# The third block's softmax transposes on VectorE instead of TensorE, and its value products two steps later

## The chip, the core and the metric

The kernel runs on one core of one Trainium2 chip. The metric is the device time of one execution in microseconds (us); the kernel before is given by the median of three runs.

## The reference

Chunked attention over chunks of 64 tokens (8 batches, 8 heads, 576 tokens of 64 values each), followed by a gated feed-forward layer over all 4608 tokens. All is float32.

```python
# q, k, v: (8, 8, 576, 64), cut into 9 chunks of 64 tokens
scores = (q_c @ k_c.transpose) / sqrt(64)
scores = scores - max(scores, axis=-1)
attn = exp(scores)
attn = attn / (sum(attn, axis=-1) + 1e-9)
x = (attn @ v_c)                      # -> (4608, 512)
g = x @ w_gate                        # (512, 1536)
val = x @ w_val                       # (512, 1536)
out = (silu(g) * val) @ w_out         # (1536, 512)
```

## The kernel before

The 4608 tokens are worked on in nine blocks of 512 (`N`), one for each chunk position over all batches. For a block, the attention gives x, held transposed as [feature, token] and split into a high part and a low part (`xh`, `xl`), so that a product is made of three reduced-precision matmuls instead of one in full float32. The feed-forward layer runs in twelve steps over slices of 128 hidden features (`NF` = 12): a gate product and a value product, silu and multiplication to h, a split of h into `hh` and `hl` (`parts`: ScalarE casts in line 62, VectorE subtracts in line 63), and the projection (`project`, lines 544 to 546), twelve matmuls of 128x512 that add into four accumulators `ps_o`.

The orders of TensorE, ScalarE and VectorE are those in which the program is written; SP's queue, which starts the loads, is ordered by a planner with its own estimates of cost, once the opening stages are past.

Blocks 0 and 1 (`a0`, `a1`) go first. While the feed-forward steps of both are computed, the h of `a1` is written to memory and its projection is left for later. The change lies in the loop that does this projection. Its steps are counted by f from 0 to 11:

```python
    for f in range(NF):
        lag(*put.pop(0))
        fetch_o(f + 3)
        extra.get(f, lambda: None)()
        if f + 2 < NF:
            put.append((prepare(f), ready_o[f]))
```

- `lag` projects the item handed over one step earlier (step 0 projects nothing, so steps 1 to 11 are twelve matmuls each).
- `fetch_o` asks for the output weights of later steps (loads of `both`).
- `prepare(f)` splits a loaded h (`h_in`) into hh and hl, each of which has two buffers, so that the split at step f waits for the buffers of the item that is projected at step f + 1; it is itself projected at step f + 3. After each odd f it asks for the next `h_in` (line 966), whose two buffers come free with the splits.
- `extra[f]` holds the work for the third block, `nxt`, whose attention is done beside this projection. Before: exponents (steps 0, 1), sums and normalizing of the pairs 0 and 1 (steps 1, 2) and 2 and 3 (steps 3, 4), the loads of the values (5), the transposes of the probabilities (6, copies of pairs 2 and 3 in step 7), the value products `columns` (8), and the split of the result into `xh` and `xl` (`first`, line 622 on ScalarE, and `rest`, line 626 on VectorE; steps 8 to 10). Step 11 computes the scores of the fourth block into the PSUM banks (`ps_gv`, `ps_a`) that the columns used. Step 6 also asks for the queries and keys of that block, behind the last load of `h_in`.

Pairs are pairs of heads; a block has four. The transpose turns probabilities [query, key] into [key, query], which the value product needs. TensorE does it by sixteen matmuls of 128x128 with an identity (`turn_to`, line 454) into PSUM, and ScalarE copies the four results to SBUF (line 1023). Later blocks of this kernel turn theirs on VectorE already (class `Attn`, `turn`, line 355), by instructions that turn eight squares of 32x32 each. `columns` (line 468) takes the pairs 0 and 1 first, then 2 and 3: 64 matmuls of 64x64 each.

After this loop, the feed-forward steps of `nxt` begin.

Of the kernel before, what the change touches and what calls it, by code (L numbers as in the profile page):

```python
# [8 lines left out]
F32 = mybir.dt.float32  # L9
# [8 lines left out]
P = 128  # L18
C = 64
# [6 lines left out]
NP = H // 2  # L26
T = 4
N = T * P
# [5 lines left out]
def attn_then_gated_ffn(ctx: ExitStack, tc: tile.TileContext, qk, v, wgv, wo, out):  # L34
    nc = tc.nc
    const = ctx.enter_context(tc.tile_pool(name="const", bufs=1))
# [7 lines left out]
    ps_gv = ctx.enter_context(tc.tile_pool(name="ps_gv", bufs=2, space=bass.MemoryType.PSUM))  # L44
    ps_o = ctx.enter_context(tc.tile_pool(name="ps_o", bufs=T, space=bass.MemoryType.PSUM))
    ps_a = ctx.enter_context(tc.tile_pool(name="ps_a", bufs=2, space=bass.MemoryType.PSUM))
# [46 lines left out]
    class Up(Narrow):  # L93
# [27 lines left out]
        def upper(self):  # L121
            f = self.f
            self.w = const.tile([P, 2, 2 * NK * P], F32R, name="w", tag=f"w{f}")
            nc.scalar.copy(out=self.w[:, 0], in_=self.t)
            w_both.append(self.w)
            w_hi.append(self.w[:, 0].rearrange("p (g k m) -> p g k m", g=2, m=P))
            w_lo.append(self.w[:, 1].rearrange("p (g k m) -> p g k m", g=2, m=P))

        def lower(self):
            nc.vector.tensor_tensor(out=self.w[:, 1], in0=self.t, in1=self.w[:, 0].bitcast(F32), op=ALU.subtract)  # L130
# [6 lines left out]
    class Quarters:  # L137
# [5 lines left out]
        def sums(self, t, s=None, engine=nc.vector):  # L143
            if s is None:
                s = const.tile([P, 4, Q], F32, name="ts", tag="ts")
            self.s = s.rearrange("p i q -> p (i q)")
            t = t.rearrange("p (i q) -> p i q", q=Q)
            engine.tensor_tensor(out=s[:, 0:2], in0=t[:, 2:4], in1=t[:, 0:3:2], op=ALU.subtract)
            engine.tensor_tensor(out=s[:, 2], in0=t[:, 3], in1=s[:, 0], op=ALU.subtract)
            engine.tensor_tensor(out=s[:, 3], in0=t[:, 1], in1=s[:, 2], op=ALU.subtract)  # L150
# [24 lines left out]
    def moved(i):  # L175
        return f"w{(i + EARLY) % NF}"
# [74 lines left out]
    class Attn:  # L251
# [83 lines left out]
        def columns(self, v_t, pT, pool=ps_a, tag="ps_a", more=False):  # L335

            pT = pT.rearrange("p (u k) -> p u k", k=C)
            px = pool.tile([P, 2 * T, C], F32, name="px", tag=tag)
            for u in range(2 * T):
                for h in range(2):  # L340
                    r = slice(h * C, (h + 1) * C)
                    nc.tensor.matmul(px[r, u, :], v_t[r, u, :], pT[r, u, :], start=not more or u == 0, stop=True,
                                     skip_group_check=more)
            return px.rearrange("p u k -> p (u k)")

        def turn(self, p, j, parts=(0, 1)):


            if not hasattr(self, "turned"):
                self.turned = const.tile([P, NP, 2, T, C], F32, name="turned", tag=self.at)  # L350
            src = self.s[:, p:p + 2].rearrange("p a c h k -> p (a c) h k")
            for i in (2 * j + i for i in parts):
                for o in range(4):
                    to = 32 * (o ^ 2 * j)
                    nc.vector.transpose(  # L355
                        out=self.turned[to:to + 32, p:p + 2, j, :, 32 * (i % 2):32 * (i % 2) + 32],
                        in_=src[32 * i:32 * i + 32, :, o // 2, 32 * (o % 2):32 * (o % 2) + 32])
# [29 lines left out]
    class First(Attn):  # L387
# [18 lines left out]
        def load_v(self, p, t):  # L406
            nc.sync.dma_start(out=t, in_=v[:, p:p + t.shape[1], self.b])

        def exchange(self, t, to, copy=nc.gpsimd.tensor_copy):
            for h in range(2):  # L410
                copy(out=to[h * C:(h + 1) * C], in_=t[(1 - h) * C:(2 - h) * C])  # L411
# [79 lines left out]
    def save_o(f):  # L491
        nc.sync.dma_start(out=kept_o[f], in_=out_now[f].bitcast(F32))
# [31 lines left out]
    def gated(a, f):  # L524
        h = gate(a, f)
        times(h, value(a, f))
        return h
# [65 lines left out]
    w, o = up[0], down[0]  # L593
# [16 lines left out]
    for a, vs in ((a0, v0), (a1, v1)):  # L610
        for c in range(2):
            pool, tag = (ld, "v_t") if a is a0 else (wp, "wo")
# [114 lines left out]
    for do in opening.split():  # L727
# [14 lines left out]
        else:  # L742
            b, i = int(do[1]), int(do[2])
# [69 lines left out]
    for f in range(1, SEVEN):  # L813
        w, o = up[f + 1], down[f]
# [168 lines left out]
    nxt = First(2)  # L983
# [15 lines left out]
    z, two, px = {}, {}, {}  # L999
# [11 lines left out]
                    r, to = slice(h * C, (h + 1) * C), slice((1 - h) * C, (2 - h) * C)  # L1011
                    nc.sync.dma_start(out=two[p][to], in_=v[r, p, nxt.b])

    def turn():
        nxt.turned = const.tile([P, NP, N], F32, name="pT", tag="turned")
        for p in range(NP):
            pt[p] = (ps_a if p < 2 else ps_gv).tile([P, T, P], F32, name="pt", tag="ps_a" if p < 2 else "ps_gv")
            nxt.turn_to(p, pt[p])
        copy(0)

    def copy(p):
        for i in (p, p + 1):
            nc.scalar.copy(out=nxt.turned[:, i], in_=pt[i].rearrange("p m k -> p (m k)"))

    def columns():
        for p in (0, 2):
# [4 lines left out]
    def first(p):  # L1031
        for i in (p, p + 1):
            upper(nxt, px[p], i)

    def rest(p):
        for i in (p, p + 1):
            lower(nxt, px[p], i)

    pt = {}
    nxt.places()  # L1040

    extra = {0: lambda: nxt.exponents(0), 1: lambda: (nxt.exponents(2), sums(0)), 2: lambda: nxt.normalize(0, z[0]),
             3: lambda: sums(2), 4: lambda: nxt.normalize(2, z[2]), 5: load_v, 6: turn, 7: lambda: copy(2), 9: lambda: (first(2), rest(0)), 10: lambda: rest(2)}

    def scores(a, beside_pair=True, at=None, tiles=None):

# [175 lines left out]
    a, pair = nxt, []  # L1222
    queries = []

    def load_queries():
        with tc.issue_after(last_fetch[0]):
            queries.extend(pair[0].a[0].load_qk(p, 1, xs, tag) for p, tag in enumerate(("xh0", "xl0", "xh1", "xl1")))
# [1 line left out]
    extra[NF - 1] = lambda: scores(pair[0].a[0], False, tiles=(queries[:2], queries[2:]))  # L1229
    ask = extra[6]  # L1230
    extra[6] = lambda: (ask(), pair.append(Pair(3, moved(2))), load_queries())
    extra[8] = columns
    save_o(NF - 1)
    for f in range(NF):
        lag(*put.pop(0))
# [6 lines left out]
    c = pair.a[0]  # L1242
# [25 lines left out]
    for i in range(NF):  # L1268
        f = (i + EARLY) % NF
        h = gated(a, f)  # L1270
# [17 lines left out]
    for b in range(3, NB, 2):  # L1288
        pair.last = b + 2 == NB
        middle, behind, bursts, later = {}, {}, {}, {}  # L1290
        if not pair.last:
            n = Pair(b + 2, moved(11))
            c = n.a[0]
# [45 lines left out]
```

## Time and profile before

| | |
|---|---|
| median of three runs | 893.55 us (893.28 to 893.56) |
| the profiled execution | 893.09 us |
| its span, from the first to the last instruction | 890.9 us |
| TensorE busy | 880.8 us (99%) |
| VectorE busy | 547.6 us (61%) |
| ScalarE busy | 388.1 us (44%) |
| granted TensorE clock, mean | 0.999 |
| the loop of the change, from its first projection to the fourth block's scores | 186.1 to 222.2 us |

The rows below name an instruction by its start in us from the start of the span, its length, its engine (PE is TensorE, PEld its weight loads, DVE is VectorE, ACT is ScalarE, SPq the loads started by SP), its line in the kernel and its tiles, `out<-in`. In brackets stands the time in which the engine stood idle before it, and what ended that. Rows for a whole line give the durations as min/median/max in ns.

### The profile page before, as it was taken

What the parts mean: (1) busy time and instruction counts of PE and PEld (TensorE: products, weight loads), DVE (VectorE), ACT (ScalarE), POOL (GpSimd) and SP (SyncE); (2) the same over time, 40 slices, a digit from 0 to 9 for tenths busy, and PEclk for the clock granted to TensorE, in tenths of its full rate; (3) what the DMA queues carried; (4) which work ended last, traced back from release to release, by engine and by line L of the source; (5) the groups of instructions that cost most, each with busy time, mean ns of one, the idle gap of its engine ahead of it and who ended that gap; (6) DMA issues with size and microseconds to landing.
All of it is one profiled execution on the core that took longest, in us unless ns stands there. A gap on an engine that the chain in (4) does not pass through costs nothing.

```text
span 890.9 us, 14750 instructions
## 1 busy us (share of the span) xinstructions
PE 880.8 (99%) x6038; PEld 729.8 (82%) x6038; DVE 547.6 (61%) x830; ACT 388.1 (44%) x592; POOL 41.6 (5%) x33
## 2 busy tenths in 40 slices
PE   7999999999999999999999999999999999999998
PEld 6788888888888888888888888888888888888886
DVE  6888999673888656776753656767655533333332
ACT  5757777544433345225325444244325432223232
POOL 1200000000145110000000000000000000000000
PEclk9999999999999999999999999999999999999999
DMA  9667778889798877657577857575658575556651
GB/s 357 265 254 287 270 282 320 336 293 341 249 365 278 275 259 234 250 215 256 207 250 284 305 199 276 196 248 219 211 213 281 177 271 201 200 196 231 237 189 47
DMA packets 73314, 223.25 MB, mean 251 GB/s; under 512 B 30752, under 2 KB 31264, under 8 KB 59040
## 3 DMA queue, kind: packets, MB, share of 16 engines
q1 hardware_dynamic: 71664, 219.57, 67.8%
q10 hardware_dynamic: 1584, 2.75, 0.9%
q8 instruction: 47, 0.77, 0.3%
q14 instruction: 19, 0.16, 0.0%
HBM read 178.78 MB, written 43.52 MB: 250 GB/s over the span
## 4 chain that ended last, share of the span: by engine, by line
PE 94%; DMA 2%; DVE 2%; ACT 1%; POOL 1%; issue 0%; SPq 0%; ACTq 0%; DVEq 0%; POOLq 0%
PE ps_a L865 26%; PE ps_gv L865 20%; PE ps_gv L478 12%; PE ps_o L544 11%; PE ps_o L546 11%; PE ps_o L545 11%; DMA v_t<-in_v 2%; PE ps_a L290 2%; PE ps_a L368 1%; DMA qk_t<-in_qk 1%; PE ps_a L468 0%; POOL v_t L411 0%; DVE h L522 0%; PE ps_a L454 0%; POOL s_sb L449 0%
## 5 line engine op out<-in xcount | busy, mean ns | idle before, releaser
L865 PE MATMUL ps_a<-x,factors 128*128 128x512 f32 x864 | 219.2, 389 | 0.0
L865 PEld LDWEIGHTS ps_a<-x,factors 128*128 128x128 f32 x864 | 162.2, 188 | 33.7
L865 PE MATMUL ps_gv<-x,factors 128*128 128x512 f32 x648 | 164.4, 389 | 0.0
L865 PEld LDWEIGHTS ps_gv<-x,factors 128*128 128x128 f32 x648 | 121.6, 188 | 25.3
L544 PE MATMUL ps_o<-both,hl 128*128 128x512 f32 (+1 forms) x337 | 132.2, 392 | 0.0
L546 PE MATMUL ps_o<-both,hh 128*128 128x512 f32 (+1 forms) x337 | 131.0, 389 | 0.0
L545 PE MATMUL ps_o<-both,hh 128*128 128x512 f32 (+1 forms) x337 | 130.9, 389 | 0.0
L63 DVE TENSOR_TENSOR hl<-h,hh 128x512 fp32r<-128x512 f32 x98 | 68.2, 696 | 65.1 <-ACT hh L62 64.9
L62 ACT CAST hh<-h 128x512 fp32r<-128x512 f32 x98 | 60.6, 618 | 95.5 <-PE ps_o L546 51.3
L478 PE MATMUL ps_gv<-xh,w 128*128 128x512 f32 x320 | 97.2, 390 | 0.1
L869 DVE TENSOR_TENSOR h<-h,ps_gv 128x512 f32<-128x512 f32 x44 | 30.2, 686 | 105.3 <-PE ps_gv L865 105.2
L355 DVE STREAM_TRANSPOSE turned<-s_sb 32x256 f32<-32x256 f32 x192 | 83.7, 436 | 2.7
L522 DVE SCALAR_TENSOR_TENSOR h<-v,h 128x512 f32<-128x512 f32 x88 | 60.9, 692 | 38.0 <-ACT h L1170 33.3
L544 PEld LDWEIGHTS ps_o<-both,hl 128*128 128x128 f32 x337 | 63.2, 188 | 13.4
L546 PEld LDWEIGHTS ps_o<-both,hh 128*128 128x128 f32 x337 | 63.3, 188 | 13.2
L545 PEld LDWEIGHTS ps_o<-both,hh 128*128 128x128 f32 x337 | 63.3, 188 | 12.8
L478 PEld LDWEIGHTS ps_gv<-xh,w 128*128 128x128 f32 x320 | 60.0, 188 | 12.7 <-ACT xh L622 0.3
L1170 ACT ACTIVATE h<-ps_a 128x512 f32<-128x512 f32 x36 | 21.5, 598 | 112.1 <-PE ps_a L865 112.1
L478 PE MATMUL ps_gv<-xl,w 128*128 128x512 f32 x160 | 61.0, 393 | 0.0
L869 DVE TENSOR_TENSOR v<-v,ps_a 128x512 f32<-128x512 f32 x44 | 30.2, 687 | 41.0 <-PE ps_a L865 36.3
L1156 ACT ACTIVATE h<-h 128x512 f32<-128x512 f32 x36 | 22.8, 632 | 52.9 <-DVE h L869 52.9
L869 DVE TENSOR_TENSOR v<-v,ps_gv 128x512 f32<-128x512 f32 x44 | 30.2, 687 | 24.2 <-PE ps_gv L865 24.2
(132 smaller groups left out, 1069.8 us busy)
## 6 DMA issues: line engine op xcount, KB each, us to landing
factors<-w SPq DMA_DIRECT2D x36, 1024.0 KB, 4.8
factors<-t SPq DMA_DIRECT2D x36, 1024.0 KB, 5.9
both<-o SPq DMA_DIRECT2D x70, 512.0 KB, 6.4
w<-w SPq DMA_DIRECT2D x16, 1024.0 KB, 7.9
t<-th SPq DMA_DIRECT2D x24, 512.0 KB, 3.6
two<-o SPq DMA_DIRECT2D x12, 1024.0 KB, 4.9
raw<-in_wgv SPq DMA_DIRECT2D x11, 1024.0 KB, 8.5
qk_t<-in_qk SPq DMA_DIRECT2D x10, 1024.0 KB, 7.6
```

What stands on the lines that cost most here:

```text
L62: nc.scalar.copy(out=hi, in_=src)
L63: (engine or nc.vector).tensor_tensor(out=lo, in0=src, in1=hi.bitcast(F32), op=ALU.subtract)
L355: nc.vector.transpose(out=self.turned[to:to + 32, p:p + 2, j, :, 32 * (i % 2):32 * (i % 2) + 32], in_=src[32 * i:32 * i + 32, :, o // 2, 3 ...
L478: nc.tensor.matmul(ps, w, x, start=first and (k, i) == which[0], stop=last and (k, i) == which[-1])
L522: nc.vector.scalar_tensor_tensor(out=h, in0=pv, scalar=2.0 ** -8, in1=h, op0=ALU.mult, op1=ALU.mult)
L544: nc.tensor.matmul(o[:, m], hl[:, ts], woh[:, m], start=f == a.steps[0], stop=False, skip_group_check=ends)
L545: nc.tensor.matmul(o[:, m], hh[:, ts], wol[:, m], start=False, stop=False, skip_group_check=ends)
L546: nc.tensor.matmul(o[:, m], hh[:, ts], woh[:, m], start=False, stop=f in (a.steps[1], a.steps[1] - final), skip_group_check=ends)
L865: nc.tensor.matmul(ps, w[u][:, k], x[i][v][:, k], start=first and k == 0 and n == 0, stop=k == NK // 2 - 1 and n == 2, skip_group_check=True)
L869: nc.vector.tensor_tensor(out=t, in0=t, in1=ps, op=ALU.add)
L1156: nc.scalar.activation(h, h, AF.Silu, scale=2.0 ** -8)
L1170: nc.scalar.activation(h2, ps1, AF.Silu, scale=2.0 ** -8)
```

## The change

The sixteen TensorE transposes and the four ScalarE copies of the third block are replaced by 32 VectorE transposes, in eight groups of four. Group i takes 32 queries of two pairs of heads: groups 0 to 3 are the pairs 0 and 1, groups 4 to 7 the pairs 2 and 3. Group 0 is placed in step 3, groups 1 to 5 in steps 5 to 9, and groups 6 and 7 in step 10. The columns move from step 8 to step 10, behind these two groups, and the split of their result, which was spread over steps 8 to 10, is now in step 10 as a whole.

```diff
-    def turn():
-        nxt.turned = const.tile([P, NP, N], F32, name="pT", tag="turned")
-        for p in range(NP):
-            pt[p] = (ps_a if p < 2 else ps_gv).tile([P, T, P], F32, name="pt", tag="ps_a" if p < 2 else "ps_gv")
-            nxt.turn_to(p, pt[p])
-        copy(0)
-
-    def copy(p):
-        for i in (p, p + 1):
-            nc.scalar.copy(out=nxt.turned[:, i], in_=pt[i].rearrange("p m k -> p (m k)"))
+    def turn(first, n=1):
+
+        if not hasattr(nxt, "turned"):
+            nxt.turned = const.tile([P, NP, N], F32, name="pT", tag="turned")
+        to = nxt.turned.rearrange("p a (c j k) -> p a c j k", j=2, k=C)
+        for i in range(first, first + n):
+            p, rows, at = i // 4 * 2, i % 4, 32 * (i % 2)
+            src = nxt.pair(p, 2).rearrange("p (n h k) -> p n h k", h=2, k=C)
+            for o in range(4):
+                nc.vector.transpose(out=to[32 * o:32 * o + 32, p:p + 2, :, rows // 2, at:at + 32],
+                                    in_=src[32 * rows:32 * rows + 32, :, o // 2, 32 * (o % 2):32 * (o % 2) + 32])
...
-    pt = {}
     nxt.places()
 
     extra = {0: lambda: nxt.exponents(0), 1: lambda: (nxt.exponents(2), sums(0)), 2: lambda: nxt.normalize(0, z[0]),
-             3: lambda: sums(2), 4: lambda: nxt.normalize(2, z[2]), 5: load_v, 6: turn, 7: lambda: copy(2), 9: lambda: (first(2), rest(0)), 10: lambda: rest(2)}
+             3: lambda: (sums(2), turn(0)), 4: lambda: nxt.normalize(2, z[2]), 5: lambda: (load_v(), turn(1)),
+             6: lambda: turn(2), 7: lambda: turn(3), 8: lambda: turn(4), 9: lambda: turn(5),
+             10: lambda: (turn(6, 2), columns(), first(2), rest(0), rest(2))}
...
-    extra[8] = columns
```

## The prediction

> **What bounds the kernel now.** I read the page first (shares, releasers), then the busy time by stretches, then the timelines of TensorE, VectorE, ScalarE and SP between 183 and 222 us, where the diff lies. Page, then stretches (the columns are PE, PEld, DVE, ACT and POOL busy, granted clock, DMA share, GB/s):
>
> ```profile
> span 890.9 us, 14750 instructions
> PE 880.8 (99%) x6038; PEld 729.8 (82%) x6038; DVE 547.6 (61%) x830; ACT 388.1 (44%) x592; POOL 41.6 (5%) x33
> 30.00:880.00 850.00, 849.74 (x5527) 703.76 (x5527) 524.22 (x784) 368.27 (x558) 34.03 (x21) 1.00 0.69 248
> ```
>
> TensorE is busy for 849.74 of the 850 us from 30 to 880, at a granted clock of 1.00. So the kernel is one string of matmuls: what is taken out of the string in the changed stage is gained to the end, and a hole torn into it is lost to the end, as no later hole exists to swallow it.
>
> The TensorE timeline around the change (start, length, line, count):
>
> ```profile
> 199.73 0.39 PE L544 MATMUL ps_o<-both,hl 128*128 128x512 f32 x1
> 202.23 0.39 PE L546 MATMUL ps_o<-both,hh 128*128 128x512 f32 x1
> 202.46 1.91 PE L454 MATMUL pt<-ident,s_sb 128*128 128x128 f32 x16
> 206.94 0.39 PE L544 MATMUL ps_o<-both,hl 128*128 128x512 f32 x1
> 209.43 0.39 PE L546 MATMUL ps_o<-both,hh 128*128 128x512 f32 x1
> 209.75 2.11 PE L468 MATMUL ps_a<-pT,v_t 64*64 64x64 f32 x128
> 211.79 0.50 PE L544 MATMUL ps_o<-both,hl 128*128 128x512 f32 x1
> 214.65 0.39 PE L544 MATMUL ps_o<-both,hl 128*128 128x512 f32 x1
> 217.14 0.39 PE L546 MATMUL ps_o<-both,hh 128*128 128x512 f32 x1
> ```
>
> A step of the loop is twelve matmuls: step 6 is the first two rows, so the pitch is (202.23 - 199.73) / 11 = 0.227 us and a step 2.72 us. Steps 7 and 9 start at 204.12 and 211.79; 206.94 starts step 8, 214.65 step 10, and 217.14 is step 10's last matmul. The reader is to see that steps follow each other without a hole even around the transposes and the columns.
>
> VectorE and ScalarE in the same stretch (the bracket is idle time before, and its releaser):
>
> ```profile
> 195.76 1.27 DVE L435 TENSOR_REDUCE z<-s_sb 128x8 f32<-128x512 f32 x2
> 197.87 0.69 DVE L63 TENSOR_TENSOR hl<-h_in,hh 128x512 fp32r<-128x512 f32 x1 [0.84 <-ACT hh L62]
> 198.97 1.23 DVE L449 TENSOR_TENSOR s_sb<-s_sb,z 128x1024 f32<-128x1024 f32 x1
> 202.49 0.69 DVE L63 TENSOR_TENSOR hl<-h_in,hh 128x512 fp32r<-128x512 f32 x1 [2.30 <-ACT hh L62]
> 218.22 0.69 DVE L63 TENSOR_TENSOR hl<-h_in,hh 128x512 fp32r<-128x512 f32 x1 [0.83 <-ACT hh L62]
> 218.83 1.28 DVE L626 TENSOR_TENSOR xl<-ps_a,xh 128x512 fp32r<-128x512 f32 x2
> 201.84 0.62 ACT L62 CAST hh<-h_in 128x512 fp32r<-128x512 f32 x1 [4.00 <-DMA h_in<-h]
> 202.66 0.62 ACT L62 CAST hh<-h_in 128x512 fp32r<-128x512 f32 x1 [0.20 <-PE ps_o L546]
> 217.56 0.62 ACT L62 CAST hh<-h_in 128x512 fp32r<-128x512 f32 x1 [1.12 <-PE ps_o L546]
> ```
>
> VectorE is half idle, but it is tied to TensorE: `prepare(f)` at step f needs the buffers of hh and hl (two each) that TensorE frees at the end of step f+1. The last row shows it: step 10 ends at 217.14 + 0.39 = 217.53, hh of `prepare(9)` starts at 217.56, hl at 218.22, and the next VectorE instruction at 218.83. So everything that the code puts behind `prepare(9)` on VectorE starts 218.83 - 217.14 = 1.69 us after step 10's last matmul started.
>
> **The change part by part.**
>
> *TensorE's sixteen transposes go.* Between 202.23 and 206.94 lie 13 pitches (2.95 us) and the transposes: 4.71 - 2.95 = 1.76 us. All on the path: -1.76 us.
>
> *What they covered.* Step 7 multiplies the hl of `prepare(4)`, which VectorE makes at 202.49 to 203.18, because its hh started at 201.84, released by the load of h_in. The transposes stood in front of that (202.46 to about 204.1). Without them step 7 wants its first matmul at 202.46; VectorE hands over at 203.18, 0.03 us go to the signal (217.53 to 217.56), and the weight load leads its matmul by 0.23 us:
>
> ```profile
> 217.14 0.19 PEld L544 LDWEIGHTS ps_o<-both,hl 128*128 128x128 f32 x1
> 217.37 0.39 PE L544 MATMUL ps_o<-both,hl 128*128 128x512 f32 x1
> 194.15 0.39 SPq L966 DMA_DIRECT2D h_in<-h  x1
> 198.59 0.32 SPq L966 DMA_DIRECT2D h_in<-h  x1
> 204.03 0.32 SPq L966 DMA_DIRECT2D h_in<-h  x1
> DMA to landing us min/median/max: 4.5/6.3/7.6
> ```
>
> So the matmul starts at 203.44: a hole of 0.98 us. The load was issued at 194.15 and took the longest of the five; nothing ahead of it in the queue is moved by the diff, so I keep 201.84. The ends: 0 (a landing 1 us sooner, well above the 4.5 us) and 0.98. I take 0.98.
>
> *ScalarE's four copies go* (line 1023, two at a time, 1.07 us a pair). They stood beside TensorE's steps, with ScalarE idle before most of its neighbours: 0.
>
> *VectorE gets 32 transposes of 32x256.* The nearest rows are this kernel's own of that shape in later stages:
>
> ```profile
> L355 DVE STREAM_TRANSPOSE turned<-s_sb x192: 425/436/442, 238.3 to 650.0; 32x256 f32<-32x256 f32 x192
> 238.29 1.77 DVE L355 STREAM_TRANSPOSE turned<-s_sb 32x256 f32<-32x256 f32 x4
> ```
>
> A group is 4 in 1.77 us (0.444 apart); two groups are 7 x 0.444 + 0.436 = 3.54 us. Groups one by one, with VectorE's next hl starting 0.61 us after the last (218.22 to 218.83):
> - Group 0, step 3: behind the sums (195.76 + 1.27 = 197.03) to 198.77; the hl of `prepare(3)` slips from 197.87 to about 198.75 and ends at 199.44. Step 6 loads it at 199.73 - 0.23 = 199.50. It just fits: 0 (ends 0 and 0.1).
> - Normalizing the second pairs slips as well and ends near 201.1, before 202.49: 0.
> - Groups 1 to 5, one a step: 1.77 + 0.61 = 2.38 us a step against TensorE's 2.72. The hl of `prepare(5)` ends near 205.6, and step 8 loads it near 205.95. Later ones gain margin. 0.
> - The h_in loads issued at 198.59 and 204.03 wait for those hl and slip by 0.9 and 1.5 us. At the median landing they are there at 205.8 and 211.9; their hh have their buffers at the ends of steps 7 and 9, 203.44 (above) + 11 x 0.227 + 0.39 = 206.3 and 5.44 later, 211.8. 0, with up to 1.4 us late for the second at a landing of 7.6.
> - Groups 6 and 7, step 10, are the ones with no cover. They stand behind `prepare(9)`, so start 1.69 us after step 10's last matmul began and end 1.69 + 3.54 = 5.23 us after it, 5.26 with the signal.
>
> *The columns move from step 8 to step 10.* Their own price stays: 214.65 - 209.43 = 5.22 less 13 pitches is 2.27 us. But half of them (pairs 2 and 3) read what group 7 writes. The first half starts 209.75 - 209.43 = 0.32 us after the last matmul and takes half of 211.79 - 209.75, so it is done after 1.34 us. TensorE then stands until 5.26: a hole of **3.92 us**. Step 11 is queued behind it, so nothing fills it. Bounds: with the fastest transposes (425 ns, back to back 3.40) 3.78; with the late h_in 1.1 us more, 5.0.
>
> *Cover of the upper and lower parts.* Both couples are now read behind the columns. From the end of the columns: two hh of line 622 and two lowers of line 626; these took 1.07 and 1.28 for two in the rows of before, overlapped about 1.9 us. The scores behind step 11 want those banks 2.72 us later. 0, margin 0.8; it costs at most the excess.
>
> *Buffers of the values* free about 5 us later. The next loads of v_t in these tiles and ScalarE's output tiles come at
>
> ```profile
> 229.81 2.05 ACT L561 ACTIVATE o_sb<-ps_o 128x512 f32<-128x512 f32 x4
> 234.38 0.71 SPq L270 DMA_DIRECT2D v_t<-in_v  x1
> ```
>
> so 0. SP's order is the planner's; the diff moves no DMA call, and I take the order as it is.
>
> **Sum.** -1.76 + 0.98 + 3.92 = +3.14 us. The profiled execution took 893.09 (span 890.9), so 896.2; it lies 0.46 under the median of 893.55, from which I give **896.7**. About 0.2% (1.8 us) is what a measurement can tell from no change.
>
> **A rule that speaks against the change.** The longest waits of TensorE now are
>
> ```profile
> PE ps_a L672 <- DVE tops L665: 2.2, 2, 1.1
> PE unread L58 <- POOL ident masks.py:199: 1.4, 1, 1.4
> 8.14 1.10 PE L672 MATMUL ps_a<-tops,minus 128*128 128x512 f32 x4 [1.12 <-DVE tops L665]
> 8.00:12.00 4.00, 3.43 (x79) 3.02 (x80) 3.40 (x8) 2.59 (x6) 0.59 (x1) 1.00 1.03 395
> ```
>
> 1.4 us at the longest, and behind the wait that ended at 8.14 the granted clock was 1.00; a hole of 3.9 us has no row here. The Trainium skill ("TensorE: Matmul & The Clock Gate", Part 1, The HAM clock gate) says that a whole idle window of about 3.4 us puts TensorE back to half clock until a busy window has passed, and that the windows run freely, so that a hole needs luck to hold a whole one. By that rule an estimate is (3.9 - 3.4) / 3.4, about one hole in seven. No run here shows it yet.
>
> **The rivals.**
> 1. *The clock drops in the hole.* If the step behind the hole, whose twelve matmuls take 2.72 us, ran at half the granted clock, it would cost 2.72 once more: 899.4. Against it: the clock of 1.00 by every wait so far, none longer than 1.4; for it, that this hole is nearly three times as long.
> 2. *Not slower: the cover holds.* If groups 6 and 7 were done before TensorE wants the second half of the columns, the hole of 3.92 vanishes and -1.76 + 0.98 = -0.78 remains: 892.8; with h_in in time too, 891.8, the most that can be gained. It decides at VectorE: 3.54 us of transposes would have to start before 1.34 - 3.54 = 2.2 us ahead of step 10's last matmul start. Against it: the row at 217.56, hh released by the end of the step, with hl and the groups behind it in written order.
> 3. *h_in late.* The load behind `prepare(5)` slips past 211.8 and pushes groups 5 to 7: +1.1, 897.8. For it: the DMA share is above 1.0 here, landings reach 7.6; against: the median fits.
>
> ```profile
> 199.70:202.45 2.75, 2.75 (x13) 2.20 (x12) 0.49 (x1) 0.61 (x1) 0.00 (x0) 1.00 1.04 425
> ```
>
> 4. *Smaller holes.* If h_in lands sooner for step 7, +2.2: 895.7, still slower; it takes a second saving of 0.4 us, in the hole of step 10, to come within 0.2%.
>
> **How the numbers follow.** Forecast (with case 4 down to 895.4) 0.58; clock 0.12; h_in late or another DMA order 0.14; cover holds 0.10; smaller holes that end within 0.2% 0.06. Slower is 0.58 + 0.12 + 0.14 = 0.84. The covered case gives -0.78, within 0.2%, and a tenth of a case beyond it with everything in time: same 0.13, faster 0.03. The range goes from 895.1 (no h_in hole, a hole of 3.5) to 899.2 (late h_in, or part of the clock's price), which leaves out about 0.2.
>
> **What would show it.** After: no L454 in this stage; step 7 about 1 us behind step 6, released by hl; 32 transposes near 436 ns, four a step, TensorE regular from step 7 to 10; the first half of the columns behind step 10, a hole of near 3.9 us released by VectorE's transpose, then the second half; step 11 at about 220.5 instead of 217.37, and the rest shifted by that. Wrong would be: a hole under 2 us, transposes done before step 10 ends, a granted clock under 1.00 behind the hole, or later holes.

## The result, and the profile after

The changed kernel takes 900.75 us (median of five runs, 899.03 to 901.24) where the kernel before takes 893.55 (893.28 to 893.79): a ratio of 1.0077, 95% interval 1.0066 to 1.0087. It is slower, as forecast, but by 7.2 us instead of 3.1, and 900.75 lies above the range of 895.1 to 899.2. The profiled execution took 899.54, which is 6.45 more than the profiled one of before; its span grew by 6.5.

The first lines of the changed kernel's page:

```profile
span 897.4 us, 14746 instructions
PE 881.6 (98%) x6022; PEld 729.6 (81%) x6022; DVE 561.3 (63%) x862; ACT 385.7 (43%) x588; POOL 41.7 (5%) x33
```

TensorE's waits in it from the list of waits (total us, times, longest):

```profile
PE ps_a L468 <- DVE pT L1023: 3.5, 2, 2.9
PE ps_o L544 <- DVE hl L63: 1.3, 1, 1.3
PE ps_gv L865 <- issue: 0.3, 1, 0.3
PE ps_o L546 <- issue: 0.3, 1, 0.3
```

TensorE runs sixteen matmuls fewer and is busy 0.8 us longer. That is the first hint: something made the remaining ones slower. The waits show the two holes that the prediction named (the columns on line 468, the projection of step 7 on line 544), and two that it did not.

The timeline of the changed stage, TensorE first, then the rows of SP, ScalarE and VectorE that explain it:

```profile
202.30 0.39 PE L546 MATMUL ps_o<-both,hh 128*128 128x512 f32 x1
203.97 0.50 PE L544 MATMUL ps_o<-both,hl 128*128 128x512 f32 x1 [1.29 <-DVE hl L63]
206.82 0.39 PE L544 MATMUL ps_o<-both,hl 128*128 128x512 f32 x1
214.76 0.39 PE L546 MATMUL ps_o<-both,hh 128*128 128x512 f32 x1
215.07 1.28 PE L468 MATMUL ps_a<-pT,v_t 64*64 64x64 f32 x72
219.29 0.33 PE L468 MATMUL ps_a<-pT,v_t 64*64 64x64 f32 x2 [2.94 <-DVE pT L1023]
220.22 1.76 PE L468 MATMUL ps_a<-pT,v_t 64*64 64x64 f32 x54 [0.60 <-DVE pT L1023]
222.50 0.63 PE L545 MATMUL ps_o<-both,hh 128*128 128x512 f32 x1
222.93 0.63 PE L546 MATMUL ps_o<-both,hh 128*128 128x512 f32 x1
225.67 2.10 PE L290 MATMUL ps_a<-qk_t 64*64 64x64 f32 x128
...
194.64 0.33 SPq L966 DMA_DIRECT2D h_in<-h  x1
202.57 1.14 ACT L62 CAST hh<-h_in 128x512 fp32r<-128x512 f32 x2 [4.72 <-DMA h_in<-h]
215.18 0.62 ACT L62 CAST hh<-h_in 128x512 fp32r<-128x512 f32 x1 [2.10 <-PE ps_o L546]
203.22 0.69 DVE L63 TENSOR_TENSOR hl<-h_in,hh 128x512 fp32r<-128x512 f32 x1 [1.97 <-ACT hh L62]
213.95 1.80 DVE L1023 STREAM_TRANSPOSE pT<-s_sb 32x256 f32<-32x256 f32 x4
215.83 0.69 DVE L63 TENSOR_TENSOR hl<-h_in,hh 128x512 fp32r<-128x512 f32 x1
216.56 3.61 DVE L1023 STREAM_TRANSPOSE pT<-s_sb 32x256 f32<-32x256 f32 x8
```

The scores of the fourth block start at 225.67. Before, they started at

```profile
220.18 1.02 PE L290 MATMUL ps_a<-qk_t 64*64 64x64 f32 x51
```

so 5.5 us are lost by there. Two matmuls behind the hole show the rest of it: they stand 0.43 us apart instead of 0.227. The stretches behind the hole show the same in the clock (the column after the five engines):

```profile
220.20:222.00 1.80, 1.78 (x55) 1.67 (x55) 1.28 (x2) 0.00 (x0) 0.00 (x0) 0.51 0.68 172
222.00:223.50 1.50, 1.50 (x4) 1.21 (x5) 0.88 (x2) 1.07 (x2) 0.00 (x0) 0.50 0.05 11
```

Half the clock was granted through both, about 3.4 us with the edges, and half of that is lost: 1.7 us. The sum at the scores is then: 1.64 of the 1.76 us lost again by step 8 (206.82 instead of 206.94), 3.9 for the hole, 1.7 for the clock, so -1.76 + 1.64 + 3.9 + 1.7 = 5.5. The last 1.0 us goes far away, in two stages that the diff doesn't touch:

```profile
490.97 0.39 PE L546 MATMUL ps_o<-both,hh 128*128 128x512 f32 x1 [0.33 <-issue]
641.02 1.43 PE L865 MATMUL ps_gv<-x,factors 128*128 128x512 f32 x5 [0.34 <-issue]
```

Here TensorE waits for nothing that the trace shows. (A matmul that should stand 0.227 us behind the one ahead of it stands later by 0.48 us at the first place; the same working gives 0.6 at the second.) The experiments ask what the clock and these far holes belong to. The edits below are shortened; `...` stands for what is left out. Theory A: the hole at the columns brings the half clock. Theory B: the clock is incidental, and the excess belongs to loads and to the VectorE groups in steps 3 to 9. For the far holes, theory C: sixteen instructions fewer shift the places at which TensorE's code is fetched. Theory D: they come of the change's loads.

### The profile page after: what moved, and what is told of

Its sections match the earlier page's. It is cut to its first block, busy times and chain, and to the rows that moved or that the text cites. A ratio compares the mean times of both kernels' runs of the same rounds, so it can differ in the third digit from the quotient of the medians.

```text
span 897.4 us, 14746 instructions
## 1 busy us (share of the span) xinstructions
PE 881.6 (98%) x6022; PEld 729.6 (81%) x6022; DVE 561.3 (63%) x862; ACT 385.7 (43%) x588; POOL 41.7 (5%) x33
## 4 chain that ended last, share of the span: by engine, by line
PE 92%; DVE 2%; DMA 2%; ACT 1%; issue 1%; POOL 0%; SPq 0%; ACTq 0%; DVEq 0%
PE ps_a L865 26%; PE ps_gv L865 19%; PE ps_gv L478 12%; PE ps_o L544 11%; PE ps_o L546 10%; PE ps_o L545 10%; PE ps_a L290 2%; PE ps_a L368 1%; DMA v_t<-in_v 1%; DMA h_in<-h 1%; DVE pT L1023 0%; PE ps_a L454 0%; PE ps_a L468 0%; ACT xh L622 0%; ACT hh L62 0%
```

## The experiments

**1. TensorE kept working through the hole.** Unread transposes fill the time between the halves of the columns:

```diff
-            px[p] = nxt.columns_of_two((two[p], two[p + 1]), nxt.turned[:, p:p + 2], ...
+            ...
+            for _ in range(28 if p else 0):
+                nc.tensor.transpose(px[p][0][:, 0:2].rearrange("p u k -> p (u k)"), ident, ident)
+            nxt.columns_to(px[p], (two[p], two[p + 1]), nxt.turned[:, p:p + 2])
```

> The changed kernel, with 28 more TensorE transposes of the identity (into a bank that the second half of the columns overwrites) placed between the two halves of the columns, so that TensorE works through most of the 3.5 us hole instead of standing idle. The hole's length stays as it was, since VectorE still sets when the second half can start. Theory A (the loss is the hole plus a halved clock that the idle time brings on): the granted clock stays 1.00, step 11 takes 2.7 us instead of 3.8, the time falls by 1.7 to 3.4 us from 900.75 to 897.3 to 899.0, and the runs lie within 0.7 us of each other. Theory B (the clock is incidental, the rest of the loss comes from loads and from holes later in the kernel): 900 to 901, with the spread of 2 us that the changed kernel showed.

Measured: 897.71 (896.83 to 899.70), ratio 1.0051 (1.0039 to 1.0064), 3.0 us less than the changed kernel. Its TensorE timeline:

```profile
216.13 3.27 PE L1031 MATMUL ps_a<-ident 128*128 128x128 f32 x28
220.18 1.04 PE L468 MATMUL ps_a<-pT,v_t 64*64 64x64 f32 x54 [0.40 <-DVE pT L1023]
224.10 2.10 PE L290 MATMUL ps_a<-qk_t 64*64 64x64 f32 x128
```

The stretch from the end of the hole on (the clock is the 1.00 behind the engines):

```profile
219.00:223.00 4.00, 3.60 (x76) 2.92 (x75) 3.51 (x7) 1.07 (x2) 0.00 (x0) 1.00 0.66 194
```

The second half starts when it did (220.18 for 220.22), so VectorE's time is the same; the clock stays at 1.00, and the scores start 1.6 us sooner. So the clock follows from TensorE standing idle, as theory A has it. Most of the rest of the gain is not the clock: the far holes are gone too, in a kernel whose TensorE stream is 28 matmuls longer. The spread did not shrink to the 0.7 us that I expected; it is 2.9, of which 1.7 stand in the spans (894.4 to 896.1); the rest lies outside them and is not explained.

**2. The hole alone, in the kernel before.** TensorE keeps its transposes in step 6; the columns move to step 10, and the eight transposes of groups 6 and 7 are done over again ahead of them:

```diff
+    def again_by_dve(first, n):
+        ...
-             ... 9: lambda: (first(2), rest(0)), 10: lambda: rest(2)}
+             ... 10: lambda: (again_by_dve(6, 2), columns(), first(2), rest(0), rest(2))}
...
-    extra[8] = columns
```

> The kernel before with its transposes on TensorE in step 6 as they were, its columns moved to step 10, and the eight VectorE transposes of groups 6 and 7 added in step 10 ahead of the columns (they write what is there already). So the hole in front of the second half of the columns is there, and nothing else of the change. Theory A: a hole of 3.5 to 3.9 us and a half clock for one or two windows behind it, 893.55 + 3.9 + 1.7 to 3.4 = 899.2 to 900.9, spread over some 2 us from run to run. Theory B (the loss beyond the hole belongs to the VectorE groups of steps 3 to 9, the late load of h_in and later holes): 897.0 to 897.7, runs close together.

Measured: 899.37 (898.59 to 900.29), ratio 1.0067 (1.0054 to 1.0080). TensorE's only wait from 30 us on:

```profile
PE ps_a L468 <- DVE pT L1045: 3.5, 2, 2.9
```

A stretch of step 11, with its clock of 0.50:

```profile
222.00:223.50 1.50, 1.50 (x5) 1.12 (x4) 1.29 (x2) 0.65 (x2) 0.00 (x0) 0.50 0.00 0
```

One wait, the same 3.5 us, the same half clock, and nothing else: this costs 6.0 us by itself (the kernel before ran beside it at 893.40), inside theory A's 899.2 to 900.9 and outside theory B's 897.0 to 897.7. The five runs fall in two lots by their mean granted clock, 0.998 (898.59, 898.67, 899.37) and 0.996 (899.81, 900.29): this fits one stretch of half clock or two. Two stretches in some runs may also be behind the spread of the changed kernel, but its five clocks (0.996 to 0.998) don't fall apart so, and only one execution of each was traced.

**3. The groups earlier.** No work is taken away; groups 1 to 7 start one or two steps earlier, and none stands behind the last split:

```diff
-             3: lambda: (sums(2), turn(0)), 4: lambda: nxt.normalize(2, z[2]), 5: lambda: (load_v(), turn(1)),
-             6: lambda: turn(2), 7: lambda: turn(3), 8: lambda: turn(4), 9: lambda: turn(5),
-             10: lambda: (turn(6, 2), columns(), first(2), rest(0), rest(2))}
+             3: lambda: (sums(2), turn(0)), 4: lambda: (nxt.normalize(2, z[2]), turn(1)), 5: lambda: (load_v(), turn(2)),
+             6: lambda: turn(3), 7: lambda: turn(4), 8: lambda: turn(5, 2), 9: lambda: turn(7),
+             10: lambda: (columns(), first(2), rest(0), rest(2))}
```

> The changed kernel with its eight groups placed earlier: 0 in step 3, 1 in step 4, 2 in step 5, 3 in step 6, 4 in step 7, 5 and 6 in step 8, 7 in step 9; the columns stay in step 10. VectorE does the same work but group 1 falls into time in which it waited for h_in, and nothing stands behind the last split. Theory A: the hole at the columns shrinks to 0.5 to 1.2 us, the clock stays 1.00, the time is 893.55 - 1.76 + 1.44 (hole of step 7) + 0.9 = 894.1, between 893.5 and 895. Theory B: only the shorter hole is gained, 900.75 - 2.6 = 898.1.

Measured: 896.65 (895.95 to 897.00), ratio 1.0035 (1.0021 to 1.0049), between the two expectations. TensorE's waits from 30 us on:

```profile
PE ps_o L546 <- issue: 1.2, 1, 1.2
PE ps_o L544 <- DVE hl L63: 1.0, 1, 1.0
PE ps_a L468 <- DVE pT L1023: 1.0, 2, 0.6
PE ps_gv L865 <- issue: 0.9, 1, 0.9
```

The stretch behind the hole at the columns:

```profile
217.40:221.30 3.90, 3.90 (x70) 3.07 (x70) 3.03 (x5) 1.08 (x2) 0.00 (x0) 1.00 1.03 297
```

The far holes in TensorE's timeline, and a burst of small matmuls ahead of the first:

```profile
480.77 2.16 PE L368 MATMUL ps_a<-turned,v_t 64*64 64x64 f32 x128
487.52 0.39 PE L546 MATMUL ps_o<-both,hh 128*128 128x512 f32 x1 [1.19 <-issue]
638.09 1.43 PE L865 MATMUL ps_gv<-x,factors 128*128 128x512 f32 x5 [0.89 <-issue]
```

In the stage itself theory A is right: the hole shrinks to 1.0 us, the clock stays at 1.00. What puts the time 2.5 us above my figure are the far holes, at the same instructions as in the changed kernel, and larger (1.35 and 1.18 us against the kernel before). Each of them comes a few us after a burst of 128 small matmuls (line 368 here), which use up TensorE's instructions more than ten times as fast as the large ones (128 in 2.16 us). Shortly ahead of the first hole, in the stretch from 485 to 486 us, the list of DMA queues shows a fetch of code (packets, MB, share of the queues' time):

```profile
q8 instruction: 1, 0.02, 6.0%
```

That alone proves nothing: the kernel before has a fetch between 484 and 485.5 us too, and no hole. Experiment 6 comes back to it.

**4. The values behind h_in.** The loads of the values (line 1008 and 1012) wait for the fourth h_in:

```diff
+    def load_v_late():
+        with tc.issue_after(last_fetch[0]):
+            load_v()
...
-             ... 5: lambda: (load_v(), turn(1)),
+             ... 5: lambda: (load_v_late(), turn(1)),
```

> The changed kernel with the loads of the third block's values (1 MB) queued behind the fourth load of h_in instead of ahead of the third, so that the third h_in meets less traffic. If the hole of step 7 (1.44 us) is made by the traffic of these loads, h_in lands before 201.5, the hole goes and the time falls by about 1.4 us from 900.75 to 899.3, as long as the clock behaves as in the changed kernel. If h_in is late for another reason, the hole stays and the time too, 900 to 901.

Measured: 901.92 (901.53 to 904.37, four runs), ratio 1.0102 (1.0088 to 1.0115): slower still. The hole of step 7 did go, since the split that it waited for now starts at 200.42, as soon as TensorE frees its buffer; and nothing was won. The timeline of ScalarE and TensorE:

```profile
200.42 0.62 ACT L62 CAST hh<-h_in 128x512 fp32r<-128x512 f32 x1 [2.10 <-PE ps_o L546]
212.58 0.62 ACT L62 CAST hh<-h_in 128x512 fp32r<-128x512 f32 x1 [3.38 <-DMA h_in<-h]
...
215.80 0.34 PE L468 MATMUL ps_a<-pT,v_t 64*64 64x64 f32 x6 [0.59 <-DVE pT L1023]
219.23 0.47 PE L468 MATMUL ps_a<-pT,v_t 64*64 64x64 f32 x2 [3.10 <-DVE pT L1023]
220.16 1.77 PE L468 MATMUL ps_a<-pT,v_t 64*64 64x64 f32 x54 [0.45 <-DVE pT L1023]
```

Two stretches behind the hole:

```profile
219.90:223.50 3.60, 3.34 (x58) 2.94 (x59) 2.42 (x5) 1.07 (x2) 0.00 (x0) 0.50 0.55 152
223.50:225.50 2.00, 2.00 (x7) 1.52 (x6) 0.35 (x1) 0.00 (x0) 0.00 (x0) 0.50 0.00 0
```

TensorE came to the columns 1.2 us sooner and waited for VectorE until the same 220.16. The traffic moved from the third h_in to the fifth, whose split now starts at 212.58, released by the load: the third rival of the prediction, made by this edit. Behind the longer hole the clock is 0.50 through both of the stretches, twice as long as in the changed kernel; the scores start at 226.55, 0.9 us later than there. Another 0.9 us goes at the second far place: line 865 waits 1.66 us there, up to 642.73 (the trace names ScalarE's line 1153). So this run doesn't tell what the hole of step 7 is worth by itself, because its edit made the fifth h_in late in its place.

**5. The missing instructions put back.** Experiment 3 with sixteen unread transposes, eight in each hole of the stage:

```diff
+            ...
+            for _ in range(8 if p else 0):
+                nc.tensor.transpose(px[p][0][:, 0:2].rearrange("p u k -> p (u k)"), ident, ident)
...
-             ... 6: lambda: turn(3), ...
+             ... 6: lambda: (keep_warm(8), turn(3)), ...
```

> The kernel with the early groups, with 16 more TensorE transposes of the identity that nobody reads: eight between steps 6 and 7 (inside the hole that waits for h_in) and eight between the halves of the columns (inside the hole there). TensorE's instruction stream then has the length of the kernel before again (6038 matmuls) from the columns on. Theory C (the two holes of 1.2 and 0.9 us near 487 and 638 us of the kernel with the early groups, put down to nothing that the trace shows, come of the place at which TensorE's instruction fetches fall against its bursts of small matmuls, which the 16 missing transposes shifted): both holes go, the rest stays, 896.65 - 2.3 = 894.3, between 893.9 and 894.9, and the fetches near them stand about as in the kernel before. Theory D (they come of other traffic or another order of loads, which the change brought with it): they stay, 896 to 897.

Measured: 894.89 (894.00 to 896.43, eleven runs), ratio 1.0018 (1.0009 to 1.0027): 1.8 us less than experiment 3, by adding work. From 226 us on the trace has no wait of TensorE at all. The loads and VectorE's groups of the change are all still there, so theory D doesn't explain the far holes; theory C holds as far as the number of instructions goes.

**6. The shift alone, in the kernel before.** Sixteen fewer of the unread transposes that the opening has anyway:

```diff
-        ... B000 B001 .6 gb S02 S03 .6 E000 ... B011 .6 E010 ... T01 .6 S11 ...
+        ... B000 B001 .2 gb S02 S03 .2 E000 ... B011 .2 E010 ... T01 .2 S11 ...
```

> The kernel before with nothing changed but 16 fewer of the unread TensorE transposes in its first 17 us (four runs of six became two each), where TensorE waits for loads anyway; everything behind has the same instructions in the same order. Theory C (place of the instruction fetches): the trace shows the same two holes near 487 and 638 us as the changed kernel, without any of its transposes on VectorE, and the time rises by 1 to 2.4 us from 893.4 to 894.4 to 895.8. Theory D (they belong to the change's loads): no such holes, 893.4 within 0.4, or a little more if the opening itself becomes slower, which its first 30 us would show.

Measured: 896.47 (895.49 to 902.88, six runs), ratio 1.0037 (1.0025 to 1.0050). That is above the 894.4 to 895.8 of theory C. But the opening itself became slower: the profiled execution, the longest of the six, is 4.8 us late by 60 us, with a long wait and 6.8 us of half clock behind it. How much of that the other five runs have isn't known, so only the places are read, not the sum. The wait of the opening:

```profile
PE ps_a L468 <- issue: 2.9, 1, 2.9
```

TensorE's timeline, where the far holes were:

```profile
490.50 0.50 PE L545 MATMUL ps_o<-both,hh 128*128 128x512 f32 x1 [0.60 <-issue]
642.50 2.20 PE L865 MATMUL ps_gv<-x,factors 128*128 128x512 f32 x6 [2.16 <-DMA v_t<-in_v]
```

Holes at both places, without a single transpose moved to VectorE (for the second the trace names a load; its place is the one of the far hole). Behind the second, of 2.16 us, the clock is halved as it is behind the hole at the columns:

```profile
643.30:646.70 3.40, 3.40 (x10) 2.63 (x9) 0.00 (x0) 0.59 (x1) 0.00 (x0) 0.50 0.37 86
```

All ten traces agree on the length of the stream: the four kernels with 6022 matmuls (the changed one and experiments 3, 4 and 6) have both holes, the first of experiment 4 being only 0.06 us long, and the six with 6030, 6038 or 6050 have neither. Lateness alone doesn't do it: experiment 2 is 5.5 us late at these places and has no hole. So the far holes need nothing of the change but its shorter stream.

The records of the code's DMA queue fit theory C further. In the four traces with holes a fetch begins 3.2 to 4.7 us after the burst of 128 small matmuls began, and the hole ends 2.2 to 2.5 us after that (in the changed kernel: burst at 485.09, fetch at 488.66, end of the hole at 490.97). In the six others a fetch begins 1.3 to 4.3 us ahead of the burst (before: 475.62 and 479.75). That TensorE waits for this code is still an inference; no run changed the fetches alone.

**7. Half of the change.** Pairs 0 and 1 on VectorE, pairs 2 and 3 on TensorE with two ScalarE copies, the columns in step 8 again, pairs 2 and 3 first. The loads of the values are moved too, behind the third h_in:

```diff
+             3: lambda: (sums(2), load_v_late(), turn(0)), 4: lambda: nxt.normalize(2, z[2]), 5: lambda: turn(1),
+             6: lambda: (turn_rest(), turn(2)), 7: lambda: turn(3), 8: lambda: columns(), 9: lambda: (first(0), rest(2)),
+             10: lambda: rest(0)}
...
```

> Half of the change: the pairs 0 and 1 are turned on VectorE (groups 0 to 3 in steps 3, 5, 6 and 7), the pairs 2 and 3 by eight TensorE transposes in step 6 with two ScalarE copies; the columns are back in step 8, pairs 2 and 3 first; the values load behind the third h_in instead of ahead of it. Worked out: eight transposes fewer are 0.88 us of TensorE; the other eight stand between steps 6 and 7, so that the hole there is at most 0.2 us; group 3 ends near 209.2, ahead of the second half of the columns at 209.9. Expected 893.4 - 0.88 = 892.5 with no new hole, up to 893.5 with part of one; if the missing eight transposes shift the instruction fetches badly, up to 2 us more at the two places near 487 and 638 us. A time above 895.5 would speak against this account.

Measured: 893.81 (892.76 to 897.27, twelve runs), ratio 1.0009 (1.0000 to 1.0017): no gain, and 0.3 us above the worked-out 892.5 to 893.5. Its profiled run, one of its fastest at 892.76, has the stage as worked out, without a hole:

```profile
202.38 1.03 PE L454 MATMUL pt<-ident,s_sb 128*128 128x128 f32 x8
208.80 2.45 PE L468 MATMUL ps_a<-pT,v_t 64*64 64x64 f32 x128
219.56 2.12 PE L290 MATMUL ps_a<-qk_t 64*64 64x64 f32 x128
```

The scores start 0.6 us sooner than before. The median doesn't keep it; the runs spread over 4.5 us, and why is open.

**8. How long a hole the clock bears.** Groups 1 to 6 one step earlier, group 7 alone left in step 10, sixteen unread transposes in step 6:

```diff
-             ... 4: lambda: nxt.normalize(2, z[2]), 5: lambda: (load_v(), turn(1)),
-             6: lambda: turn(2), 7: lambda: turn(3), 8: lambda: turn(4), 9: lambda: turn(5),
-             10: lambda: (turn(6, 2), columns(), ...
+             ... 4: lambda: (nxt.normalize(2, z[2]), turn(1)), 5: lambda: (load_v(), turn(2)),
+             6: lambda: (keep_warm(16), turn(3)), 7: lambda: turn(4), 8: lambda: turn(5), 9: lambda: turn(6),
+             10: lambda: (turn(7), columns(), ...
```

> The changed kernel with the groups one step earlier, so that only group 7 stands in step 10 behind the last split, and with 16 unread TensorE transposes between steps 6 and 7 that keep the length of TensorE's stream. The hole at the columns should be near 2 us (one group, 1.77, less than in the changed kernel). If a hole of 2 us leaves the clock at 1.00: 893.4 + 2.0 + about 0 (the transposes of 1.76 are back in place of the hole of step 7) = 895.3, runs within 0.7 us. If it also brings a half clock for a window: 1.7 us more, 897, with a spread of 2 us.

Measured: 897.05 (896.67 to 897.39), ratio 1.0041 (1.0029 to 1.0053).

TensorE's timeline:

```profile
217.51 0.33 PE L468 MATMUL ps_a<-pT,v_t 64*64 64x64 f32 x2 [1.15 <-DVE pT L1023]
218.44 1.25 PE L468 MATMUL ps_a<-pT,v_t 64*64 64x64 f32 x54 [0.60 <-DVE pT L1023]
```

The stretch behind:

```profile
219.00:222.50 3.50, 3.50 (x40) 2.80 (x30) 1.99 (x4) 1.07 (x2) 0.00 (x0) 0.51 0.59 168
```

A hole of 1.15 and 0.60 us is enough for 3.4 us of half clock; one of 1.0 in all (experiment 3) was not. All five runs of each agree by their mean clock (0.998 here, 0.999 to 1.000 there). Whether it also matters when a hole falls was not tried. The second branch of the expectation holds in its sum, and its spread was overstated (0.7 us).

## Why the prediction was wrong, step by step

- *Sixteen transposes, -1.76 us*: right (the step after them starts where the sum puts it, once the hole is taken off).
- *What they covered, 0.98 us*: the mechanism was right, the size off. The load was issued at 194.64 instead of 194.15 and landed in time for 202.57 instead of 201.84; with small slips the cost by step 8 was 1.64, 0.66 more than the term. I had kept the landing of one execution; the wait itself was 1.29 us here, 1.2 in experiment 1 and 1.0 in experiment 3. What would be gained by taking it away stays open: in experiment 4 it went and nothing was won, but there the fifth h_in came late and VectorE's end stayed where it was.
- *VectorE's 32 transposes*: right in their length. Eight took 3.61 us (3.54 predicted), and the hole ended 220.22 - 214.76 = 5.46 us after step 10's last matmul began (5.26 predicted). But the margin of groups 1 to 5 was not there: a step of VectorE took 2.52 us instead of 2.38 ((215.83 - 203.22) / 5), the first came late with h_in, and VectorE worked without a wait from 203.22 to 220.17. Group 5 ended at 215.75, the last hh at 215.80: the last split waited for both alike. That the forecast end came out is partly luck.
- *The hole of 3.92 us at the columns*: right in place, cause and size (2.94 + 0.60 idle, beside eight matmuls of the second half that could go ahead).
- *The clock, first rival, 0.12*: the step that failed. It is part of what the hole costs: 1.7 us for a stretch of half clock (the rival had 2.72). I put it at nothing in the sum, by the trace, whose longest wait was 1.4 us at a clock of 1.00, and by how seldom a hole of 3.9 us would hold a whole window of 3.4. It came every time: all five runs of the changed kernel and all five of experiment 2 have a mean clock of 0.998 or less, the kernel before 0.999 or more. The Trainium skill ("TensorE: Matmul & The Clock Gate", Part 1, The HAM clock gate) puts the half clock down to at least one idle window of about 3.4 us. The traces bear out the half clock and a duration of about 3.4 us; that it takes a whole idle window they do not, for 1.75 us of idle time did it in experiment 8. By the measurement the clock belonged in the sum, at 893.55 + 3.14 + 1.7 = 898.4.
- *The clock alone doesn't leave the range*: 898.4 lies below 899.2. The 0.66 us more at step 7 and the 1.0 us of the far holes (below) bring it to 900.1, and with them the profiled executions agree (3.14 + 1.7 + 0.66 + 1.0 = 6.5, measured 6.45). The last 0.7 us of the median stand in no trace.
- *The lower end of the range*: its own terms, -1.76 and a hole of 3.5, give 895.3, not 895.1. Nothing hangs on it here.
- *"Or later holes"*, named only as what would be wrong: no step priced what it does to the rest of the kernel that sixteen matmuls leave TensorE's stream. They cost 1.0 us here and 1.8 to 2.5 in experiment 3, far from the edit.
- *Cover of the upper and lower parts, buffers of the values, ScalarE's copies, at nothing*: no wait of that kind stands in the trace.

## What to carry to other kernels

Work taken off a full engine gains only if its replacement ends before that engine asks for it; here eight transposes behind the last split cost 5.6 us against a gain of 1.76, and the same groups one step earlier left a hole of 1.0 us. A hole in TensorE of two us is priced with the clock that follows it, not by its length alone. And a change in the number of instructions ahead of a tight stage can open holes far behind it, so look at the whole trace for waits, not only at the edited stage.

## What the runs showed of the hardware that was not expected

- The half clock came behind 1.75 us of idle TensorE within 2.1 us (experiment 8) and behind a single hole of 2.16 us (experiment 6), lasted about 3.4 us, and cost 1.7; a hole of 1.0 us in two parts did not bring it (experiment 3), and 28 unread transposes in the hole kept it away (experiment 1).
- TensorE's stream length matters by itself: sixteen matmuls fewer gave holes of 0.06 to 2.16 us at two fixed places, some 280 and 430 us behind the edit in the changed kernel, and sixteen unread ones took 1.8 us off the median. Each hole ended 2.2 to 2.5 us after a fetch of code began.
